# First MLP products inside the last pair of heads, and the first quarter of features in chunks of 384 tokens

## The chip, the cores and the metric

The kernel runs on one core of one Trainium2 chip. The metric is the time of one execution on the device in microseconds (us), median of several runs. TensorE (PE) multiplies into PSUM; VectorE (DVE), ScalarE (ACT) and GpSimd (POOL) do the elementwise work; SyncE's queue (SP) issues the DMAs. Each engine takes its instructions in order, and semaphores tie the engines to each other.

## The reference

Inputs are q, k and v of shape (2, 8, 768, 64), 16 centroids for each head, and two pairs of weight matrices of 512 x 2048 and 2048 x 512, all in float64. What is computed, cut to its core:

```
q_assign = argmax(q_n . c_n); k_assign = argmax(k_n . c_n)      # nearest of 16 centroids
scores = where(q_assign == k_assign, (q . k) / 8, -1e9)          # 768 x 768 for each of 16 heads
attn = softmax(scores) @ v                                       # (2, 8, 768, 64)
x = attn as (1536 tokens, 512)
h = relu(x @ w1_in); x = (h * h) @ w1_out                        # first MLP
h = x @ w2_in; x = (h * clip(h + 3, 0, 6) / 6) @ w2_out          # second MLP
```

## The kernel before

Attention goes by pairs of heads (a "unit", `NU` = 8: two batches of four pairs). A pair has 12 query tiles of 128 rows. For tile n, PE makes the scores `s` (L593, L596), DVE their maximum `nm` (L602), ACT the exponent `e` (L613); PE transposes `e` into `t` in two halves (L629), each is split into a rounded part `eh` and a rest `el` (either ACT L639 and DVE L640, or by way of a copy `et` on POOL, L154 and L637; the table `ON_POOL` says which), and for each three tiles PE multiplies `eh` and `el` with v into `a` (L656). The two halves of `a` are added in `emit_u` (ACT `tmp`, DVE `u`, L670); there is one buffer for `a`, so the next three tiles' product waits for that sum. Every float32 operand is such a sum of two, so an exact product is three matmuls.

The order in attention is written out by hand (`schedule`, within `tc.manual_schedule()`): tile n emits its transposes, the exponent of n+1 and the scores of n+2, and the tables `STEPS`, `FIRST`, `WEIGHTS`, `WEIGHTS_7` and `AV` put each preparing step of each pair at a place (tile, slot 0 to 4). Beside the tiles run the preparing steps of the next pair (transposes of q and k, clusters, one-hot `oh` and its transposed mask `toh` L459, the splitting of v) and the decoding of the first quarter of `w1_in`, one of eight pieces in a pair and two in the last.

The weights come as float64 and are decoded in seven instructions (`decode`): POOL clamps `t` (L167), ACT scales `u` (L169), DVE does three integer steps (L172, L174, L179), ACT rounds the high part (L183), and the low part is on POOL for the first quarter and on DVE for the others (L185).

The MLPs take 2048 features in four quarters and 1536 tokens in three chunks of 512. `mm1` makes 4 x 12 products of 512 columns and their gate (ACT `r` L842, `g` L843, POOL `gh` L154, DVE `gl` L848); `mm2` makes 4 x 12 products with the second matrix. The steps go mm1(0), mm1(1), mm2(0), mm1(2), mm2(1), and so on. `load_w` decodes a matrix in four pieces of 128 rows, with one buffer each for `t`, `u` and `a` and two for the raw `wr`; outside attention a scheduler sets the order at build time. The first of these is the first quarter of `w1_out`: its four pieces are decoded from the end of attention on, and mm2(0) needs all four.

Of the kernel before, what the change touches and what calls it, by code (L numbers as in the profile page):

```python
# [38 lines left out]
    "v0": (-6, 4),  # L39
    "v1": (-1, 2),  # L40
# [11 lines left out]
        "v0": (1, 4),  # L52
# [4 lines left out]
        "load v": (-6, 4),  # L57
        "k0": (-12, 2),
# [5 lines left out]
        "stack1": (-10, 3),  # L64
# [33 lines left out]
TMP_DVE = ()  # L98
BIG = float(2**60)
# [5 lines left out]
def cluster_attention_mlp_kernel(  # L105
# [50 lines left out]
    def decode(pool, hi, lo, r, on_dve):  # L156
# [42 lines left out]
    with ExitStack() as actx:  # L199
# [63 lines left out]
        def first_weights():  # L263
# [3 lines left out]
            def half(c, h):  # L267
# [19 lines left out]
            return [half(c, h) for c in range(4) for h in range(2)]  # L287
# [37 lines left out]
        def prep(u):  # L325
# [9 lines left out]
            def transp(x, half):  # L335
# [42 lines left out]
            def sims(half, x):  # L378
# [12 lines left out]
                if u == 0:  # L391
                    steps.insert(1, (C0, "H"))
# [5 lines left out]
                if x == 1 and u == 0:  # L398
# [27 lines left out]
            def leader(r0=0, r1=R, i=None):  # L426
# [9 lines left out]
                (nc.gpsimd if u else nc.vector).tensor_tensor(  # L436
# [3 lines left out]
            def onehot(r0=0, r1=R, i=None):  # L440
# [9 lines left out]
                nc.vector.tensor_tensor(  # L450
# [25 lines left out]
            def vsplit(half):  # L476
# [5 lines left out]
                pool_round(tt[:, :, 0:D], vr)  # L482
                nc.gpsimd.tensor_sub(tt[:, :, D:], vr, f(tt)[:, :, 0:D])
# [134 lines left out]
        def emit_tr(n, half):  # L618
# [27 lines left out]
        def emit_av(g, part):  # L646
# [7 lines left out]
            for kr in (2 * part, 2 * part + 1):  # L654
# [43 lines left out]
        def emit_norm(u, half):  # L698
# [20 lines left out]
            pool_round(XH[:, j, xs], xx)  # L719
            nc.gpsimd.tensor_sub(XL[:, j, xs], xx, f(XH)[:, j, xs])  # L720
# [13 lines left out]
        def schedule():  # L734
# [20 lines left out]
            for g in range(NTL // 3):  # L755
                for part in range(3):
# [32 lines left out]
    TC = 512  # L789
    NC = NT // TC  # L790
    NF = FQ // P
    ND = DM // P
    with ExitStack() as mctx:
        t_p = mctx.enter_context(tc.tile_pool(name="t", bufs=2, reuse_waits="tile"))
        g_p = mctx.enter_context(tc.tile_pool(name="g", bufs=2, reuse_waits="tile"))
# [3 lines left out]
        acc_p = mctx.enter_context(tc.tile_pool(name="acc", bufs=1, reuse_waits="tile"))  # L799
# [20 lines left out]

        acc = acc_p.tile([P, NC, 4, 512], F32, name="acc")
        G = {}

        def mm1(m, fq, c):
            wh, wl = wts[m, fq, 0]
            gh = g_p.tile([P, NF, TC], F32R, tag="gh", name="gh")
            gl = g_p.tile([P, NF, TC], F32R, tag="gl", name="gl")
            cs = slice(c * TC, c * TC + TC)
            for fb in range(NF):
                fs = slice(fb * P, fb * P + P)  # L830
                h = ps_h.tile([P, TC], F32, tag="h", name="h")
                n = 0
                for d in range(ND):
                    for w, x in ((wh, XH), (wh, XL), (wl, XH)):
                        nc.tensor.matmul(  # L835
                            h, w[:, d, fs], x[:, d, cs], start=(n == 0), stop=(n == 3 * ND - 1)
                        )
                        n += 1
                r = t_p.tile([P, TC], F32, tag="r", name="r")
                g = t_p.tile([P, TC], F32, tag="g", name="g")  # L840
                if m == 0:
                    nc.scalar.activation(r, h, AF.Relu)  # L842
                    nc.scalar.activation(g, r, AF.Square)  # L843
                else:
                    nc.scalar.activation(r, h, AF.Relu, bias=three)  # L845
# [91 lines left out]
```

## Time and profile before

| | |
|---|---|
| median of 3 runs | 811.45 us (810.27 to 814.22) |
| the profiled execution | 810.54 us, span 808.8 us |
| PE busy | 781.5 us, 97% of the span |
| DVE, ACT, POOL busy | 530.1, 395.8, 344.0 us |
| attention | 0 to 283.56 us of the span |
| both MLPs | 283.56 us to the end |

A busy PE is not PE at its peak: matmuls overlap, so their mean duration is longer than the time from one start to the next. A row of busy time by stretch gives the stretch, its length, the busy time of PE, PE's weight loads, DVE, ACT and POOL with their instructions, the granted clock as a share of 2.4 GHz (0.5 is 1.2 GHz), and the share and rate of the DMAs. Shares over the span mean little here, since attention and the MLPs have different limits; the rows below are read by stage.

### The profile page before, as it was taken

Reading aid. Unit: us, or ns where it says so; the run is one execution under the profiler, and the core shown is the slowest. Engines: PE = TensorE matmul, PEld = TensorE weight load, DVE = VectorE, ACT = ScalarE, POOL = GpSimd, SP = SyncE. Lnnn points to the kernel's source line nnn. Section 1 sums busy time; section 2 is a strip of 40 time slices with the busy share of each in tenths; the row PEclk is TensorE's granted clock in tenths of the full one; section 3 lists DMA queues with packets and bytes.
Section 4 is the critical chain, followed back from the end, with each engine's and each line's share of the span. In section 5 each row is a group of like instructions: output and inputs, shape, how many; then the busy total and the mean of one; then the engine's idle time right before and its main releaser. Section 6 shows DMA issues by size and latency. Waiting matters only on the chain.

```text
span 808.8 us, 11331 instructions
## 1 busy us (share of the span) xinstructions
PE 781.5 (97%) x3973; PEld 664.1 (82%) x3973; DVE 530.1 (66%) x877; ACT 395.8 (49%) x784; POOL 344.0 (43%) x461
## 2 busy tenths in 40 slices
PE   7999999999998699999999999999999999999998
PEld 6888888888987688888888888888888888888887
DVE  6888889898886666655766455576654666643432
ACT  5888888887886555545434334331333222311110
POOL 1778887888787552233322122333222221211110
PEclk9999999999999999999999999999999999999999
DMA  8837538448350123333222121121221211000012
GB/s 179 175 87 168 130 71 199 92 109 182 69 123 15 57 77 103 104 104 101 77 83 79 40 92 52 53 79 52 79 79 41 89 53 53 26 1 1 13 47 97
DMA packets 58536, 67.34 MB, mean 83 GB/s; under 512 B 41320, under 2 KB 41744, under 8 KB 58480
## 3 DMA queue, kind: packets, MB, share of 16 engines
q1 hardware_dynamic: 58480, 66.62, 30.8%
q8 instruction: 32, 0.52, 0.3%
q14 instruction: 24, 0.20, 0.1%
HBM read 43.02 MB, written 3.15 MB: 57 GB/s over the span
## 4 chain that ended last, share of the span: by engine, by line
PE 82%; POOL 5%; DVE 5%; issue 3%; ACT 2%; DMA 1%; SPq 1%; ACTq 0%; POOLq 0%
PE o L868 32%; PE h L835 32%; PE a L656 5%; PE t L629 4%; PE s L593 2%; PE s L596 2%; POOL el L637 2%; DVE nm L602 2%; PE tsim L394 2%; PE tq L349 1%; POOL eh L154 1%; DVE el L640 1%; DMA rawq<-in_q_dram 1%; DVE a L174 1%; DVE xx L718 1%
## 5 line engine op out<-in xcount | busy, mean ns | idle before, releaser
L835 PE MATMUL h<-xh,w 128*128 128x512 f32 x768 | 240.3, 389 | 0.0
L835 PEld LDWEIGHTS h<-xh,w 128*128 128x128 f32 x768 | 144.2, 188 | 29.7
L154 POOL TENSOR_SCALAR gh<-g 128x512 fp32r<-128x512 f32 x96 | 73.9, 769 | 194.1 <-DVE g L846 136.1
L835 PE MATMUL h<-xl,w 128*128 128x512 f32 x384 | 149.6, 390 | 0.0
L868 PE MATMUL o<-w,gh 128*128 128x512 f32 (+1 forms) x392 | 120.3, 385 | 0.0
L868 PE MATMUL o<-gh,w 128*128 128x512 f32 x384 | 120.2, 389 | 0.0
L167 POOL TENSOR_SCALAR t<-wr 128x512 f32<-128x512 f32 (+1 forms) x68 | 48.1, 707 | 161.9 <-DVE w L185 160.5
L183 ACT ACTIVATE w<-t 128x512 fp32r<-128x512 f32 (+1 forms) x68 | 41.2, 605 | 129.0 <-DVE t L179 90.6
L629 PE MATMUL t<-ident,e 128*128 128x128 f32 x576 | 93.6, 276 | 10.0 <-ACT e L613 8.4
L637 POOL TENSOR_TENSOR el<-et,eh 128x384 fp32r<-128x384 f32 x96 | 97.3, 1013 | 7.9
L848 DVE TENSOR_TENSOR gl<-g,gh 128x512 fp32r<-128x512 f32 x96 | 66.4, 693 | 51.5 <-POOL gh L154 51.5
L602 DVE TENSOR_REDUCE nm<-s 128x1 f32<-128x768 f32 x96 | 90.7, 946 | 2.2 <-PE s L596 2.2
L613 ACT ACTIVATE e<-s,nm 128x768 f32<-128x768 f32 x96 | 86.5, 901 | 5.3 <-DVE nm L602 5.3
L629 PEld LDWEIGHTS t<-ident,e 128*128 128x128 f32 x576 | 71.0, 141 | 21.5 <-ACT e L613 13.5
L169 ACT ACTIVATE u<-t 128x512 f32<-128x512 f32 (+1 forms) x68 | 41.3, 607 | 93.4 <-POOL t L167 93.4
L868 PEld LDWEIGHTS o<-w,gh 128*128 128x128 f32 x392 | 73.2, 188 | 14.7
L835 PEld LDWEIGHTS h<-xl,w 128*128 128x128 f32 x384 | 72.1, 188 | 14.9
L868 PEld LDWEIGHTS o<-gh,w 128*128 128x128 f32 x384 | 72.1, 188 | 14.9
L845 ACT ACTIVATE r<-h,three 128x512 f32<-128x512 f32 x48 | 32.6, 682 | 89.9 <-PE h L835 89.9
L868 PE MATMUL o<-w,gl 128*128 128x512 f32 (+1 forms) x196 | 75.4, 385 | 0.0
L172 DVE TENSOR_SCALAR a<-u 128x512 int32<-128x512 int32 (+1 forms) x68 | 30.9, 454 | 67.6 <-ACT u L169 67.6
L868 PE MATMUL o<-gl,w 128*128 128x512 f32 x192 | 74.7, 389 | 0.0
(121 smaller groups left out, 1298.5 us busy)
## 6 DMA issues: line engine op xcount, KB each, us to landing
wr<-in_moe_w_out_dram SPq DMA_DIRECT2D x32, 512.0 KB
wr<-in_moe_w_in_dram SPq DMA_DIRECT2D x28, 512.0 KB
op<-H SPq DMA_DIRECT2D x56, 192.0 KB
op<-L SPq DMA_DIRECT2D x28, 192.0 KB
rawv<-in_v_dram SPq DMA_DIRECT2D x16, 192.0 KB
out_dram<-acc SPq DMA_DIRECT2D x11, 256.0 KB
rawq<-in_q_dram SPq DMA_DIRECT2D x14, 192.0 KB
rawk<-in_k_dram SPq DMA_DIRECT2D x14, 192.0 KB
```

The source lines that it names most:

```text
L154: nc.gpsimd.tensor_scalar(dst, src, 1.0, 0.0, op0=ALU.mult, op1=ALU.add)
L167: nc.gpsimd.tensor_scalar(t, f(hw), MOST, -MOST, op0=ALU.min, op1=ALU.max)
L169: nc.scalar.activation(u, t, AF.Copy, scale=2.0**-112)
L183: nc.scalar.activation(hi, t, AF.Copy)
L602: nc.vector.tensor_reduce(nm, S_t[n][:, :, :HS], axis=AX.XY, op=ALU.max, negate=True)
L613: nc.scalar.activation(e, s[:, :, :HS], AF.Exp, bias=nm, accum_out=sums[u][:, i * R + r : i * R + r + 1])
L629: nc.tensor.transpose(t[:, c, :], E_t[n][:, half, c * P : (c + 1) * P], ident)
L637: nc.gpsimd.tensor_sub(el, et, f(eh))
L656: nc.tensor.matmul(a[:, :HS], vs[:, kr, i, :], x[:, kr, :], start=(kr == 0 and x is eh), stop=(kr == R - 1 and x is el),)
L835: nc.tensor.matmul(h, w[:, d, fs], x[:, d, cs], start=(n == 0), stop=(n == 3 * ND - 1))
L848: nc.vector.tensor_sub(gl[:, fb], g, f(gh)[:, fb])
L868: nc.tensor.matmul(o, lhsT, rhs, start=(n == 0), stop=(n == 3 * NF - 1))
```

## The change

The first 384 tokens' products with the first quarter of `w1_in` (4 blocks of 12 products, and their gates) are emitted among the tiles of the last pair, at the places of `EARLY`. The first quarter of features then goes by four chunks of 384 tokens. The steps are now early(0); mm1(384); mm1(768), mm2(0), mm2(384); mm1(1152), mm2(768); mm1 of the next quarter; and so on. Half the columns of all four row blocks of `w1_in` are decoded first. In all pairs the step `u` of this decoding is on DVE; the last two pieces have their clamp and low part on DVE and `u` on ACT. The last pair has its own `ON_POOL_LAST` (9 halves on POOL instead of 12, four of whose copies are on DVE); the other pairs have 11 instead of 12. H and L are one tile, and the accumulator lies by features for the first MLP and by tokens for the second. The switches `E_...` and `SIM3` other than `E_U` stand as the code was. Slots of the preparing steps move by one or two tiles at most.

```
+    "load v": (-12, 4),
...
-WEIGHTS = ((0, 4), (3, 0), (4, 0), (5, 0), (5, 3), (7, 1), (7, 4), (9, 1))
+WEIGHTS = ((0, 2), (3, 4), (4, 4), (6, 0), (6, 3), (7, 3), (9, 3), (10, 0))
...
-    ((-2, 4), (0, 2), (0, 4), (1, 3), (2, 2), (3, 3), (3, 4), (4, 1)),
+    ((-1, 3), (0, 0), (0, 4), (1, 1), (1, 3), (1, 4), (2, 0), (2, 0)),
...
-AV = ((4, 0), (4, 4), (5, 2))
+LATE = {(2, 1), (3, 1)}
+EARLY = (
+    ((2, 1), (2, 4), (3, 1)),
+    ((5, 3), (5, 4), (6, 1)),
+    ((7, 1), (7, 4), (9, 0)),
+    ((9, 1), (10, 1), (10, 4)),
+)
+
+AV = ((3, 3), (3, 4), (4, 4), (5, 0), (5, 2), (5, 2))
...
 ON_POOL = {
-    (0, 0), (0, 1), (1, 1), (2, 1), (3, 1), (4, 1), (6, 0), (7, 0), (9, 0), (9, 1), (10, 0),
-    (11, 1),
+    (0, 0), (1, 0), (1, 1), (2, 1), (4, 0), (4, 1), (6, 0), (7, 0), (9, 0), (9, 1), (11, 1),
...
-ET_DVE = {
-    (2, 0), (5, 0), (7, 1), (10, 0), (10, 1),
+ET_DVE = set()
+ON_POOL_LAST = {
+    (0, 0), (2, 0), (4, 0), (5, 0), (6, 1), (8, 0), (8, 1), (9, 0), (10, 0),
 }
+ET_DVE_LAST = {
+    (2, 0), (5, 0), (6, 1), (10, 0),
+}
...
-        nc.gpsimd.tensor_scalar(t, f(hw), MOST, -MOST, op0=ALU.min, op1=ALU.max)
+        (nc.vector if clamp_on_dve or not on_dve and E_CLAMP == "v" else nc.gpsimd).tensor_scalar(
+            t, f(hw), MOST, -MOST, op0=ALU.min, op1=ALU.max
+        )
         yield
-        nc.scalar.activation(u, t, AF.Copy, scale=2.0**-112)
+        if on_dve or E_U == "a":
+            nc.scalar.activation(u, t, AF.Copy, scale=2.0**-112)
+        else:
+            nc.vector.tensor_scalar(u, t, 2.0**-112, None, op0=ALU.mult)
...
-        (nc.vector if on_dve else nc.gpsimd).tensor_sub(lo, t, f(hi))
+        (nc.vector if on_dve or E_LO == "v" else nc.gpsimd).tensor_sub(lo, t, f(hi))
...
-            return [half(c, h) for c in range(4) for h in range(2)]
+            return [half(c, h) for h in range(2) for c in range(4)]
...
-            if (n % (2 * R), half) in ON_POOL:
+            if (n % (2 * R), half) in (ON_POOL if u < NU - 1 else ON_POOL_LAST):
-                copy((n % (2 * R), half) in ET_DVE, et, t)
+                copy((n % (2 * R), half) in (ET_DVE if u < NU - 1 else ET_DVE_LAST), et, t)
...
-            for kr in (2 * part, 2 * part + 1):
+            for kr in (part,):
...
+        def emit_early(fb, part):
+
+            if early[0] is None:
+                g = hl_p.tile([P, 2, NF, HS], F32R, tag="HL", name="g0")
+                early[0] = (g[:, 0], g[:, 1])
+            if part == 0:
+                early[1][fb] = ps_t.tile([P, 512], F32, tag="t", name="h0")
+            h = early[1][fb][:, :HS]
+            if part < 2:
+                for d in (2 * part, 2 * part + 1):
+                    products(h, w_first[:, 0], w_first[:, 1], fb, d, slice(0, HS))
+            else:
+                t = raw_p.tile([P, 2, HS], F32, tag="raw" + "qk"[fb % 2], name="rg")
+                gate(0, h, t[:, 0], t[:, 1], early[0][0][:, fb], early[0][1][:, fb])
...
+            for fb, places in enumerate(EARLY):
+                for part, w in enumerate(places):
+                    at(w, T * (NU - 1), partial(emit_early, fb, part))
...
+                n = HS if (m, fq) == (0, 0) else TC
+                steps += [(m, fq, c, n) for c in range(0, NT, n)]
...
             if s:
+                mm1(m, fq, c, n)
+            if s == 2:
+                mm2(*steps[0])
+            if s > 1:
                 mm2(*steps[s - 1])
```

`products` holds the three matmuls of one row block of `mm1`, and `gate` the four instructions of its gate; `emit_early` calls both.

On POOL, in the last pair, around the two halves of the pair before that are rounded there (`xh`, `xl`); `wr` and `w` are the first quarter's raw and decoded weights. Before:

```order
L637 TENSOR_TENSOR el<-et,eh 128x3x128
L154 TENSOR_SCALAR xh<-xx 128x384
L720 TENSOR_TENSOR xl<-xx,xh 128x384
L185 TENSOR_TENSOR w_68<-t,w_68 128x256
L154 TENSOR_SCALAR eh<-et 128x3x128
L637 TENSOR_TENSOR el<-et,eh 128x3x128
L154 TENSOR_SCALAR xh<-xx 128x384
L720 TENSOR_TENSOR xl<-xx,xh 128x384
L167 TENSOR_SCALAR t<-wr_3793 128x256
L154 TENSOR_SCALAR eh<-et 128x3x128
L637 TENSOR_TENSOR el<-et,eh 128x3x128
```

Now (`g` is the gate's rounded part of the early products):

```order
L178 TENSOR_SCALAR g_3751<-rg 128x384
L178 TENSOR_SCALAR eh<-et 128x3x128
L694 TENSOR_TENSOR el<-et,eh 128x3x128
L178 TENSOR_SCALAR xh<-xx 128x384
L780 TENSOR_TENSOR xl<-xx,xh 128x384
L178 TENSOR_SCALAR xh<-xx 128x384
L780 TENSOR_TENSOR xl<-xx,xh 128x384
L178 TENSOR_SCALAR eh<-et 128x3x128
L694 TENSOR_TENSOR el<-et,eh 128x3x128
L178 TENSOR_SCALAR g_3751<-rg 128x384
L178 TENSOR_SCALAR eh<-et 128x3x128
```

The low part and the clamp of the weights, which stood between the two, are gone from POOL, and a gate's rounding stands there.

On ACT, across the end of attention (`tmp` is the half of `a` that frees its buffer, `rb` the last pair's row factors, `u<-t 128x512` and `w<-t 128x512` the first piece of `w1_out`). Before:

```order
L613 ACTIVATE e,sums<-s,nm 128x768
L639 ACTIVATE eh<-t 128x3x128 x2
L169 ACTIVATE u<-t 128x512
L151 ACTIVATE tmp<-a 64x384
L151 ACTIVATE et<-t 128x384
L151 ACTIVATE tmp<-a 64x384
L710 ACTIVATE rb<-ri 128x384
L183 ACTIVATE w<-t 128x512
L710 ACTIVATE rb<-ri 128x384
L169 ACTIVATE u<-t 128x512
L842 ACTIVATE r<-h 128x512
L843 ACTIVATE g<-r 128x512
```

Now:

```order
L696 ACTIVATE eh<-t 128x3x128
L175 ACTIVATE tmp<-a 64x384
L696 ACTIVATE eh<-t 128x3x128
L175 ACTIVATE tmp<-a 64x384
L767 ACTIVATE rb<-ri 128x384
L196 ACTIVATE u<-t 128x512
L767 ACTIVATE rb<-ri 128x384
L238 ACTIVATE r<-h 128x384
L239 ACTIVATE g<-r 128x384
L238 ACTIVATE r<-h 128x384
L239 ACTIVATE g<-r 128x384
L212 ACTIVATE w<-t 128x512
```

The first piece's `u` stood ahead of both `tmp` and now stands behind both; two whole gates (`r`, `g`) now stand ahead of its `w`.

On PE, where the second products begin (`o`, one of four blocks of 128 features; `g0` is the early gate). Before:

```order
L868 MATMUL o_4446<-gl_4291,w_4143 128x512
L868 MATMUL o_4446<-gh_4290,w_4143 128x512 x2
L868 MATMUL o_4446<-gl_4291,w_4143 128x512
L868 MATMUL o_4446<-gh_4290,w_4143 128x512
L868 MATMUL o_4460<-gh_4290,w_4143 128x512
L868 MATMUL o_4460<-gl_4291,w_4143 128x512
L868 MATMUL o_4460<-gh_4290,w_4143 128x512 x2
```

Now:

```order
L231 MATMUL h_4473<-xh_63,w0_68 128x384
L937 MATMUL o_4492<-g0_3751,w_4189 128x384 x9
L937 MATMUL o_4506<-g0_3751,w_4189 128x384 x9
L937 MATMUL o_4492<-g0_3751,w_4189 128x384 x2
L937 MATMUL o_4506<-g0_3751,w_4189 128x384 x2
L937 MATMUL o_4492<-g0_3751,w_4189 128x384
L937 MATMUL o_4506<-g0_3751,w_4189 128x384
L937 MATMUL o_4520<-g0_3751,w_4189 128x384 x12
L937 MATMUL o_4534<-g0_3751,w_4189 128x384 x12
```

Nine products of the second block now stand ahead of the last three of the first, which need the fourth piece of `w1_out`.

## Rows read from the trace of the kernel before

**Rows 1.** Page, part 1: busy time of each engine

```profile
PE 781.5 (97%) x3973; PEld 664.1 (82%) x3973; DVE 530.1 (66%) x877; ACT 395.8 (49%) x784; POOL 344.0 (43%) x461
```

**Rows 2.** Busy time by stretch: a middle pair, the last stretch, the MLPs

```profile
193.93:226.08 32.15, 30.69 (x205) 27.88 (x204) 27.98 (x48) 27.21 (x62) 26.93 (x36) 1.00 0.56 127
226.08:283.56 57.48, 47.04 (x280) 41.86 (x278) 41.30 (x68) 38.47 (x87) 41.32 (x55) 0.94 0.21 56
283.56:808.00 524.44, 522.23 (x2318) 432.70 (x2317) 298.80 (x469) 173.50 (x290) 130.11 (x171) 1.00 0.20 64
```

**Rows 3.** Busy time by stretch, within the last stretch

```profile
249.24:252.44 3.20, 3.20 (x11) 3.16 (x12) 2.58 (x4) 1.70 (x4) 1.51 (x2) 0.51 0.00 0
...
262.52:265.83 3.31, 0.00 (x1) 0.00 (x0) 0.10 (x1) 1.73 (x5) 2.16 (x4) 1.00 0.00 0
265.83:269.53 3.70, 3.70 (x14) 3.56 (x15) 2.17 (x4) 2.19 (x5) 2.26 (x3) 0.54 0.00 0
...
274.83:283.56 8.73, 6.31 (x38) 5.41 (x36) 6.01 (x9) 3.48 (x8) 6.64 (x9) 1.00 0.33 113
```

**Rows 4.** Waits, 226.08 to 283.6 us: total, times, longest us

```profile
ACT u L169 <- POOL t L167: 6.3, 3, 2.9
PE t L629 <- ACT e L613: 6.1, 3, 3.3
...
PE a L656 <- DVE u L670: 2.1, 1, 2.1
```

**Rows 5.** Chain of waits, 255 to 284 us: start us, us, what

```profile
261.02 1.01 POOL el L637
...
262.59 0.99 POOL xl L720
...
263.67 0.41 POOL t L167
...
264.90 0.89 ACT e L613 x2
```

**Rows 6.** Timeline of ACT, end of attention: start us, us, what, [idle before <-releaser]

```profile
274.83 0.91 ACT L613 ACTIVATE e<-s,nm 128x768 f32<-128x768 f32 x1
...
278.87 0.63 ACT L169 ACTIVATE u<-t 128x512 f32<-128x512 f32 x1 [1.81 <-POOL t L167]
```

**Rows 7.** Timeline of PE, products of 384 and of 512 columns, first second product

```profile
281.06 0.34 PE L656 MATMUL a<-el,vs 128*128 128x384 f32 x1
...
281.75 0.33 PE L656 MATMUL a<-el,vs 128*128 128x384 f32 x1
...
302.06 0.62 PE L835 MATMUL h<-xh,w 128*128 128x512 f32 x2
...
304.10 0.62 PE L835 MATMUL h<-xh,w 128*128 128x512 f32 x2
...
305.00 0.39 PE L868 MATMUL o<-gh,w 128*128 128x512 f32 x1
```

**Rows 8.** Timeline of DVE: low parts of the first and fourth piece of w1_out

```profile
285.21 0.69 DVE L185 TENSOR_TENSOR w<-t,w 128x512 fp32r<-128x512 f32 x1 [0.38 <-ACT w L183]
...
303.83 0.69 DVE L185 TENSOR_TENSOR w<-t,w 128x512 fp32r<-128x512 f32 x1
```

**Rows 9.** Waits, 97.5 to 226.08 us (four middle pairs): total, times, longest us

```profile
PEld L459 <- DVE oh L450: 5.6, 4, 1.4
```

**Rows 10.** Groups by line and form: out<-in xcount | busy us, mean ns

```profile
L639 ACT ACTIVATE eh<-t 128x384 fp32r<-128x384 f32 x96 | 47.0, 489 | 16.0 <-PE t L629 13.9
...
L179 DVE SCALAR_TENSOR_TENSOR t<-u,a 128x512 int32<-128x512 int32 x60 | 46.9, 782 | 3.4 <-DVE a L174 0.5
...
L174 DVE SCALAR_TENSOR_TENSOR a<-wr,a 128x512 int32<-128x512 int32 x60 | 41.8, 697 | 1.3
...
L172 DVE TENSOR_SCALAR a<-u 128x512 int32<-128x512 int32 x60 | 26.4, 440 | 67.6 <-ACT u L169 67.6
...
L174 DVE SCALAR_TENSOR_TENSOR a<-wr,a 128x256 int32<-128x256 int32 x8 | 8.3, 1034 | 0.0
```

More of the change, by code (lines that the diff above doesn't have):

```diff
@@ L38 @@
     "mask": (-5, 4),
-    "v0": (-6, 4),
-    "v1": (-1, 2),
+    "v0": (-5, 2),
+    "v1": (-3, 4),
     "rinv": (11, 0),
@@ L98 @@
 TMP_DVE = ()
+ET_DVE_LAST = {
+    (2, 0), (5, 0), (6, 1), (10, 0),
+}
+SIM3 = False
+E_OH = "v"
+E_W = "p"
+E_CLAMP = "p"
+E_LO = "p"
+E_U = "v"
+E_VH = "p"
+E_VL = "p"
+E_XH = "p"
+E_XL = "p"
 BIG = float(2**60)
@@ L193, in w_src, with products, gate @@
         return w.rearrange("(c p) f -> p c f", p=P)
+    TC = 512
+    NF = FQ // P
+    ND = DM // P
+    def products(h, wh, wl, fb, d, cs):
+        fs = slice(fb * P, fb * P + P)
+        for n, (w, x) in enumerate(((wh, XH), (wh, XL), (wl, XH))):
+            nc.tensor.matmul(
+                h, w[:, d, fs], x[:, d, cs],
+                start=(d == 0 and n == 0), stop=(d == ND - 1 and n == 2),
+            )
+    def gate(m, h, r, g, gh, gl):
+        if m == 0:
+            nc.scalar.activation(r, h, AF.Relu)
+            nc.scalar.activation(g, r, AF.Square)
+        else:
+            nc.scalar.activation(r, h, AF.Relu, bias=three)
+            nc.vector.scalar_tensor_tensor(g, r, 6.0, h, op0=ALU.min, op1=ALU.mult)
+        pool_round(gh, g)
+        nc.vector.tensor_sub(gl, g, f(gh))
     w0_p = ctx.enter_context(tc.tile_pool(name="w0", bufs=1))
@@ L397, in sims @@
                     )
-                if x == 1 and u == 0:
+                if x == 1 and (u == 0 or SIM3):
                     nc.scalar.activation(st["sim"][:, hs], t[0:64, :HS], AF.Copy)
@@ L755, in schedule @@
             for g in range(NTL // 3):
-                for part in range(3):
+                for part in range(6):
                     at(AV[part], 3 * g, partial(emit_av, g, part))
@@ L819, in load_w, with mm1, mm2 @@
             wts[m, fq, which] = (hi, lo)
-        acc = acc_p.tile([P, NC, 4, 512], F32, name="acc")
-        G = {}
-        def mm1(m, fq, c):
+        acc = acc_p.tile([P, 4, NT], F32, name="acc")
+        acc1 = acc.rearrange("p d t -> p (d t)").rearrange("p (b n) -> p b n", n=DM)
+        G = {(0, 0, 0): early[0]}
+        def mm1(m, fq, c0, n):
             wh, wl = wts[m, fq, 0]
-            gh = g_p.tile([P, NF, TC], F32R, tag="gh", name="gh")
-            gl = g_p.tile([P, NF, TC], F32R, tag="gl", name="gl")
-            cs = slice(c * TC, c * TC + TC)
+            gh = g_p.tile([P, NF, TC], F32R, tag="gh", name="gh")[:, :, :n]
+            gl = g_p.tile([P, NF, TC], F32R, tag="gl", name="gl")[:, :, :n]
             for fb in range(NF):
-                fs = slice(fb * P, fb * P + P)
-                h = ps_h.tile([P, TC], F32, tag="h", name="h")
-                n = 0
+                h = ps_h.tile([P, TC], F32, tag="h", name="h")[:, :n]
                 for d in range(ND):
[L834 to L845, printed above, removed]
-                    nc.vector.scalar_tensor_tensor(g, r, 6.0, h, op0=ALU.min, op1=ALU.mult)
-                pool_round(gh[:, fb], g)
-                nc.vector.tensor_sub(gl[:, fb], g, f(gh)[:, fb])
-            G[m, fq, c] = (gh, gl)
-        def mm2(m, fq, c):
+                    products(h, wh, wl, fb, d, slice(c0, c0 + n))
+                r = t_p.tile([P, TC], F32, tag="r", name="r")[:, :n]
+                g = t_p.tile([P, TC], F32, tag="g", name="g")[:, :n]
+                gate(m, h, r, g, gh[:, fb], gl[:, fb])
+            G[m, fq, c0] = (gh, gl)
+        def mm2(m, fq, c0, n):
             wh, wl = wts[m, fq, 1]
-            gh, gl = G.pop((m, fq, c))
+            gh, gl = G.pop((m, fq, c0))
             last = fq == FF // FQ - 1
@@ L856, in mm2 @@
                 ds = slice(db * P, db * P + P)
-                end = last and m == 1 and (c, db) == (NC - 1, 3)
-                for ns in (slice(0, 256), slice(256, 512)) if end else (slice(0, 512),):
+                end = last and m == 1 and (c0 + n, db) == (NT, 3)
+                if m == 0:
+                    pieces = (slice(0, n),)
+                else:
+                    pieces = (slice(0, 256), slice(256, 512)) if end else (slice(0, 512),)
+                for ns in pieces:
                     o = ps_o.tile([P, 512], F32, tag="o", name="o")[:, ns]
-                    n = 0
+                    k = 0
                     for fb in range(NF):
@@ L889, in mm2 @@
                         )
-        steps = [(m, fq, c) for m in range(2) for fq in range(FF // FQ) for c in range(NC)]
+        steps = []
+        for m in range(2):
+            for fq in range(FF // FQ):
+                n = HS if (m, fq) == (0, 0) else TC
+                steps += [(m, fq, c, n) for c in range(0, NT, n)]
         load_w(0, 0, 1)
-        for s, (m, fq, c) in enumerate(steps):
+        for s, (m, fq, c, n) in enumerate(steps):
             if c == 0:
```

84 lines of the change are left out of this document (45 added, 39 removed).

## Prediction

> **What bounds the kernel now.** I read the page first: PE is busy for 97% of the span [rows 1], so only PE's own work and the few microseconds in which it stands still can give time back. The table by stretch says where these are [rows 2]. From 283.56 us on, PE is busy for 522.23 of 524.44 us: the MLPs are bound by PE alone. In a middle pair it is busy for 30.69 of 32.15 us. In the last stretch, 226.08 to 283.56 us, it is busy for 47.04 of 57.48 us at a mean clock of 0.94: 10.4 us without work. Within it [rows 3] there is a gap of 3.31 us, two stretches of 3.20 and 3.70 us at half clock (0.51 and 0.54, the 1.2 GHz level; the second follows the gap directly), and the tail from 274.83 us. The slow stretches cost 3.20 x 0.49 + 3.70 x 0.46 = 3.3 us, so 13.7 us could be had there.
>
> The waits tell why [rows 4]: ACT stood 6.3 us for POOL's clamp of the weights (L167), and PE 6.1 us for exponents behind it on ACT. The chain shows one such case whole [rows 5]: POOL works off a pair's rest `el` and the rounding `xh`, `xl` of the pair before, only then comes the clamp at 263.67, and ACT, which takes its list in order, starts the next exponent at 264.90. In the tail ACT waits again, 1.81 us, for the clamp of the first piece of `w1_out`, with the copy `tmp` behind it that frees PE's accumulator [rows 6]; PE then waits 2.1 us for DVE's `u` [rows 4].
>
> **The change part by part.** *Products moved.* One product of 512 columns takes (304.10 - 302.06) / 9 = 0.2267 us, one of 384 takes (281.75 - 281.06) / 4 = 0.1725 us [rows 7]. The MLPs have 2304 products, 522.3 us. Now 2016 of them keep 512 columns (457.0 us) and 384 have 384 (66.2 us): 0.9 us more in all. But 48 of these, 8.3 us, go into attention. What PE has to do after attention falls by 522.3 - 457.0 - 66.2 + 8.3 = **7.4 us**.
>
> *The last pair.* Removed from POOL there: three of twelve halves (0.5 + 1.0 us each), two clamps and two low parts; added: four gate roundings. The clamp that ACT waited for [rows 5] is on DVE now, and the order shows nothing left between `xl` and the next half on POOL but a gate's rounding. Of PE's 13.7 us I leave a middle pair's share idle, (32.15 - 30.69) / 32.15 x 57 = 2.6 us, and 1.2 us for the last wait for `u`, which remains, though `tmp` no longer stands behind the clamp. That gives 9.9 us back, and 8.3 us of new products go in: attention ends **1.6 us** earlier. The bounds are wide: all 13.7 us back would be 5.4 us earlier, nothing back 8.3 us later. A second reckoning agrees: DVE, the next engine, gets three more `el`, three more copies and four `gl` (0.55 us each, as for ACT's 0.489 [rows 10] or a little more), two clamps and two low parts (some 0.4): 7.1 us on its 41.3 [rows 2]. At a middle pair's share of 27.98 / 32.15 = 0.87, 48.4 us of DVE take 55.6 us, 1.9 less than now. Between ends so far apart I take the value from PE.
>
> *A wait added: the first piece of `w1_out`.* Before, its `u` ran at 278.87 [rows 6], before attention's end, and its low part was done at 285.21 + 0.69 = 285.90, 2.3 us after that end; the fourth was done at 303.83 + 0.69 = 304.52 [rows 8], and the second products began at 305.00 [rows 7]. They were just in time. Now `u` stands behind the last `tmp` and a row factor, so it starts about 1.1 us after the end of attention (two ACT instructions of 0.489) and takes 0.63; three integer steps of 0.44, 0.70 and 0.78 [rows 10], with one product for the last pair between, bring it to 4.2; the two gates that now stand ahead of `w` on ACT (four of 0.489) end there too; `w`, a `gl` and the low part end at 6.0, or 3.7 later than before. The three further pieces took 304.52 - 285.90 = 18.6 us beside seven gates of 512; with narrower gates I take 17.4. The fourth is done at 23.4, its high part 0.8 earlier at 22.6. PE comes sooner: 86 products (ten of the 96 fill the last wait of attention in the new order), six transposes (0.6, an estimate from the 384 columns each three cover) and the 18 second products that don't need the fourth piece make 14.8 + 0.6 + 3.1 = 18.5. So PE stands for 4.1 us where it stood for none, with everything of both MLPs behind it. A slow clock may follow: after 3.31 us of rest PE lost 1.7 us, after the 2.1 us in the tail the clock stayed at 1.00 [rows 3]. I count 1.3: **5.4 us** lost. Bounds: 0 if the pieces come in time, 9 if each takes a microsecond longer and the clock falls. Later matrices have the time of three chunks each, so I cost them at nothing.
>
> *Steps in other slots, all pairs.* The list of DVE around the one-hot is nearly what it was; the shift of a weight piece (1.034 us [rows 10]) stands behind the one-hot now and the scaling `u` (some 0.4 us) ahead of it. PE waits 1.4 us for it in each pair [rows 9]. If 0.6 us of this goes in six pairs, 3.6 us; since the shift then delays the next maximum, I take half, **1.8 us** earlier. Bounds: 8.4 us earlier (all of it), 2.5 us later (0.42 us more on DVE in each). The products with v in six steps, one tile for H and L, and the accumulator's new order change neither an instruction's size nor what PE waits for; cover is PE's own queue, and without it a move is worth one product, 0.17 us.
>
> The sum: -7.4 - 1.6 + 5.4 - 1.8 = -5.4 us on the profiled execution's 810.54 us (span 808.8 and 1.7 around it): **805.2 us**. That execution was 0.9 us under the median of the runs, 811.45, so the same sum on the median is 806.0.
>
> **The rivals.** (a) *The decoding keeps up.* It did before, with 0.5 us to spare [rows 7, 8]; if the gates of 384 let the pieces pass in 4 us, nothing is lost there: 805.2 - 5.4 = 799.8. Against it: the first piece starts 3.7 us later.
> (b) *The early products push instead of filling.* Their weights' last piece is finished within the same tiles, each holds one of the three buffers that the transposes use, and their gates stand ahead of exponents on ACT. If only half of the 9.9 us comes back, 810.2: no change.
> (c) *DVE becomes the bound of the last pair; slower than before.* The 256-element shift in attention takes 1.034 us, longer than twice as many elements in the MLPs (0.697) [rows 10], so DVE already loses time beside a busy POOL. Six moved instructions, four `gl` and two low parts, may lose a POOL instruction of 1.0 us each [rows 5], and each `gl` waits in DVE's list for POOL's rounding, 1.5 us behind a half there. Then DVE has 41.3 + 7.1 + 6 + 6 = 60.4 us, at 0.87 that is 69.4 us, attention ends 11.9 us later instead of 1.6 earlier, and the time is 818.7. It is slower by over 0.5% from an end of attention at 292.2 us on. For it speaks DVE's share; against it, that DVE had 16 us free in this stretch.
> The Trainium skill ("SBUF — State Buffer", section "SBUF: two separate sides") says that a Vector instruction with two SBUF inputs and a GpSimd instruction that reads SBUF share one pair of ports as an exclusive lock, so that the loser waits for the whole instruction. By that rule all six would be exposed, and (c)'s first 6 us would be real; the trace's 1.034 against 0.697 agrees with it, as a mean.
> (d) *The slots give more:* the whole wait for the one-hot goes, 805.2 - 6.6 = 798.6.
>
> **How the numbers follow.** Chances: forecast 0.50 (its own range 801.5 to 808.5), (a) 0.20, (b) 0.16, (c) 0.09, (d) 0.05. I call 0.5% (4.1 us) what can be told from no change: faster is below 807.4, slower above 815.5. Faster: 0.41 of the forecast's 0.50, with (a) and (d): 0.66. Same: the rest of the forecast and (b): 0.25. Slower: (c), 0.09. The range from 797.5 to 811 leaves out (c) and the ends of (a) and (d).
>
> **What would show it.** In the profile after: attention's last product with v at about 282 us; 48 products `h0` between the tiles of the last pair and no wait of ACT for POOL's clamp there; a gap of about 4 us on PE some 18 us after that, ended by ACT's `w` of the fourth piece, with a clock near 0.5 behind it; PE without gaps from there on; a middle pair of 31.5 to 32.2 us. The prediction is wrong in its main term if that gap is under 1 us or over 7, in its second if attention ends before 278 or after 287 us, and in its fourth if a middle pair differs by more than 0.8 us.

## The result and the profile after

The changed kernel takes 803.33 us (median of 4 runs, 801.34 to 805.96), the kernel before in the same session 811.55 us: ratio 0.9896, 95% interval 0.9855 to 0.9938. The forecast was 805.2 (806.0 on the median), so sign and rough size are right; the parts are not. The medians lie 8.2 us apart, the profiled executions only 4.6: that of the changed kernel, 805.96 us (span 804.3), was the slowest of its four. The parts are those of the two profiled executions:

| part of the span | forecast | measured |
|---|---|---|
| start to the last one-hot mask (slots) | -1.8 | 232.17 to 227.35: -4.8 |
| from there to the last product with v | -1.6 | 51.39 to 51.16: -0.2 |
| from there to the end (MLPs) | -7.4 + 5.4 = -2.0 | 525.2 to 525.8: +0.6 |
| sum | -5.4 | -4.5 |

The kernel before from its last one-hot mask to its last product with v:

```profile
232.17:283.56 51.39, 42.11 (x247) 37.54 (x247) 35.24 (x58) 33.36 (x75) 35.48 (x48) 0.93 0.13 39
```

The table by stretch of the changed kernel (stretch, length, busy PE, weight loads, DVE, ACT, POOL, clock, DMA) answers to [rows 2, 3]. Two middle pairs, the last pair, the MLPs' first products, the stretch with two gaps, and what follows it:

```profile
102.51:133.38 30.87, 30.65 (x204) 27.77 (x203) 27.57 (x49) 26.99 (x62) 25.39 (x34) 1.00 0.63 133
164.43:196.58 32.15, 31.10 (x204) 27.67 (x203) 27.50 (x49) 26.98 (x62) 25.37 (x34) 1.00 0.55 124
227.35:278.51 51.16, 48.29 (x301) 44.01 (x300) 39.81 (x70) 36.58 (x82) 30.98 (x41) 1.00 0.12 37
278.51:294.45 15.94, 15.94 (x93) 15.38 (x93) 11.11 (x18) 10.09 (x20) 9.08 (x11) 1.00 0.21 67
294.45:302.03 7.58, 3.83 (x20) 2.87 (x19) 5.67 (x10) 3.73 (x8) 3.03 (x4) 0.96 0.30 83
302.03:306.00 3.97, 3.97 (x12) 3.97 (x13) 2.39 (x4) 0.63 (x1) 0.66 (x1) 0.50 0.29 106
306.00:315.00 9.00, 9.00 (x46) 8.74 (x46) 3.15 (x6) 3.80 (x8) 0.64 (x1) 0.87 0.33 100
```

A middle pair takes 30.87 us where it took 32.15: PE no longer stands there. (The pair from 164.43 on is as long as before; in it PE stood for the next pair's mask, see experiment 3.) In the last pair PE is busy for 48.29 of 51.16 us and the clock is full, yet it is no shorter. After attention PE has no gap until 294.45; then it stands twice, and the clock falls to the 1.2 GHz level. PE's timeline (start, us, what, idle before and releaser) shows both waits, for `w` of the third and the fourth piece of `w1_out`:

```profile
278.34 0.34 PE L713 MATMUL a<-el,vs 128*128 128x384 f32 x1
...
294.45 1.20 PE L937 MATMUL o<-g,w 128*128 128x384 f32 x6
296.75 2.73 PE L937 MATMUL o<-g,w 128*128 128x384 f32 x12 [1.10 <-ACT w L212]
302.03 1.33 PE L937 MATMUL o<-g,w 128*128 128x384 f32 x3 [2.54 <-ACT w L212]
```

In the kernel before the second products began at 305.00 us, just behind the fourth piece [rows 7, 8], and PE was busy for 522.23 of the MLPs' 524.44 us [rows 2]. ACT's timeline shows the first piece as the prediction had it: `u` behind `tmp` and a row factor, then two gates, then `w`, 5.0 us after attention's end:

```profile
278.71 0.49 ACT L175 ACTIVATE tmp<-a 64x384 f32<-64x384 f32 x1 [4.10 <-PE a L713]
279.10 0.51 ACT L767 ACTIVATE rb<-ri 128x384 f32<-128x384 f32 x1
279.51 0.62 ACT L196 ACTIVATE u<-t 128x512 f32<-128x512 f32 x1
...
281.99 0.53 ACT L239 ACTIVATE g<-r 128x384 f32<-128x384 f32 x1
...
283.51 0.63 ACT L212 ACTIVATE w<-t 128x512 fp32r<-128x512 f32 x1
```

### The profile page after: what moved, and what is told of

Read it like the earlier page. It is cut to its first block, busy times and chain, and to the rows that moved or that the text cites. A ratio compares the mean times of both kernels' runs of the same rounds, so it can differ in the third digit from the quotient of the medians.

```text
span 804.3 us, 11576 instructions
## 1 busy us (share of the span) xinstructions
PE 784.9 (98%) x4069; PEld 676.4 (84%) x4069; DVE 531.7 (66%) x897; ACT 396.6 (49%) x794; POOL 324.9 (40%) x441
## 4 chain that ended last, share of the span: by engine, by line
PE 82%; DVE 4%; DMA 4%; ACT 3%; POOL 3%; issue 2%; SPq 2%; ACTq 0%; DVEq 0%; POOLq 0%
PE o L937 33%; PE h L231 30%; PE a L713 6%; PE t L686 5%; DMA op<-HL 3%; PE s L650 3%; PE s L653 2%; PE tsim L446 1%; SPq L298 1%; DVE nm L659 1%; POOL el L694 1%; ACT et L175 1%; DVE el L697 1%; DMA op<-mt 1%; PE tq L401 1%
## 5 line engine op out<-in xcount | busy, mean ns | idle before, releaser
L231 PE MATMUL h<-xh,w 128*128 128x512 f32 (+1 forms) x800 | 245.3, 382 | 0.5 <-ACT et L175 0.5
L231 PEld LDWEIGHTS h<-xh,w 128*128 128x128 f32 x800 | 149.3, 188 | 27.0 <-ACT et L175 0.7
L231 PE MATMUL h<-xl,w 128*128 128x512 f32 (+1 forms) x400 | 152.3, 381 | 0.0
L178 POOL TENSOR_SCALAR gh<-g 128x512 fp32r<-128x512 f32 (+1 forms) x96 | 70.5, 734 | 193.9 <-DVE g L242 133.5
L937 PE MATMUL o<-gh,w 128*128 128x512 f32 (+1 forms) x384 | 115.2, 376 | 0.0
L244 DVE TENSOR_TENSOR gl<-g,gh 128x512 fp32r<-128x512 f32 (+1 forms) x96 | 65.2, 680 | 54.5 <-POOL gh L178 54.5
L694 POOL TENSOR_TENSOR el<-et,eh 128x384 fp32r<-128x384 f32 x86 | 89.1, 1036 | 7.2
L231 PEld LDWEIGHTS h<-xl,w 128*128 128x128 f32 x400 | 75.1, 188 | 13.0
L713 PE MATMUL a<-eh,vs 128*128 128x384 f32 x192 | 71.2, 371 | 1.2 <-DVE u L727 1.2
L937 PE MATMUL o<-gl,w 128*128 128x512 f32 (+1 forms) x192 | 72.1, 376 | 0.0
```

The costliest lines, as they stand in the source:

```text
L178: nc.gpsimd.tensor_scalar(dst, src, 1.0, 0.0, op0=ALU.mult, op1=ALU.add)
L231: nc.tensor.matmul(h, w[:, d, fs], x[:, d, cs], start=(d == 0 and n == 0), stop=(d == ND - 1 and n == 2),)
L244: nc.vector.tensor_sub(gl, g, f(gh))
L694: nc.gpsimd.tensor_sub(el, et, f(eh))
L713: nc.tensor.matmul(a[:, :HS], vs[:, kr, i, :], x[:, kr, :], start=(kr == 0 and x is eh), stop=(kr == R - 1 and x is el),)
L937: nc.tensor.matmul(o, lhsT, rhs, start=(k == 0), stop=(k == 3 * NF - 1))
```

## The experiments

Each median stands beside that of the kernel before from the same session; "last stretch" is from the last one-hot mask to the last product with v.

**1. The shift back ahead of the one-hot.**

```
-WEIGHTS = (..., (4, 4), (6, 0), (6, 3), (7, 3), ...)
+WEIGHTS = (..., (4, 4), (5, 0), (5, 3), (7, 3), ...)
```

> The changed kernel with one edit: the two integer steps of the weight piece stand where they stood before the change, so that the shift (DVE a<-wr) is ahead of the one-hot again in each middle pair; nothing else moves. Theory A (the shift's place is what made PE wait for the one-hot): the wait of some 1.2 us returns in each of six pairs, a middle pair takes about 32.0 us instead of 30.8, and the time is 5 to 7 us over the changed kernel. Rival B (the wait went because u left ACT and POOL has one half fewer): a middle pair stays at 30.8 us and the time within 1 us.

Measured: 803.85 us (ratio 0.9908, 0.9878 to 0.9937), the changed kernel's time; a middle pair takes 30.84 us. My theory fell in this kernel: the shift ahead of the one-hot costs nothing.

```profile
132.95:163.79 30.84, 30.73 (x204) 27.76 (x203) 27.86 (x49) 26.86 (x62) 25.36 (x34) 1.00 0.58 134
```

**2. The same move alone, in the kernel before.**

```
-WEIGHTS = (..., (4, 0), (5, 0), (5, 3), (7, 1), ...)
+WEIGHTS = (..., (4, 0), (6, 0), (6, 3), (7, 1), ...)
```

> The kernel before with one edit: the two integer steps of the weight piece at the changed kernel's places, the shift behind the one-hot. Theory A: a middle pair falls from 32.15 to about 31 us, and the time is 5 to 7 us under the kernel before (about 805.5). Rival B: no change from 811.5.

Measured: 807.39 beside 811.02 us (ratio 0.9952, 0.9932 to 0.9972), a middle pair 31.34 us, 0.8 less. There the place does count, though for less than the 5 to 7 us of theory A. In the trace the last stretch became 1.9 us longer, at a mean clock of 0.87 instead of 0.93:

```profile
133.92:165.26 31.34, 30.84 (x205) 27.79 (x204) 27.32 (x48) 26.98 (x62) 26.57 (x36) 1.00 0.56 124
227.96:281.27 53.31, 44.99 (x248) 40.60 (x248) 35.92 (x59) 34.21 (x77) 36.37 (x49) 0.87 0.17 49
```

Between the two kernels the difference lies in how long the shift ahead of the one-hot is. In the kernel before, on POOL and DVE:

```profile
132.43 1.05 POOL L720 TENSOR_TENSOR xl<-xx,xh 128x384 fp32r<-128x384 f32 x1
```
```profile
132.58 1.19 DVE L174 SCALAR_TENSOR_TENSOR a<-wr,a 128x256 int32<-128x256 int32 x1
...
135.13 0.56 DVE L450 TENSOR_TENSOR oh<-iota,mn 128x384 bf16<-128x384 f32 x1
```

The shift starts 0.15 us into POOL's `xl` and ends 0.29 after it. In experiment 1 it starts just ahead of `xl`, and takes 0.41; it is POOL's instruction that is stretched a little:

```profile
130.56 0.41 DVE L203 SCALAR_TENSOR_TENSOR a<-wr,a 128x256 int32<-128x256 int32 x1
```
```profile
130.72 1.13 POOL L780 TENSOR_TENSOR xl<-xx,xh 128x384 fp32r<-128x384 f32 x1
```

**5. The shift one place up, in the kernel before.** This tests the collision by itself: the shift stays ahead of the one-hot but meets another POOL instruction.

```
-WEIGHTS = (..., (4, 0), (5, 0), (5, 3), (7, 1), ...)
+WEIGHTS = (..., (4, 0), (5, 0), (5, 2), (7, 1), ...)
```

> The kernel before with one edit: the shift of the weight piece one place up in DVE's list, ahead of the rest el instead of behind it; it is still ahead of the one-hot. Theory A (the shift is long only because it starts while POOL's xl runs and has to wait for the end of it; one place up it starts beside xh): the shift takes some 0.41 us instead of 1.19, a middle pair some 31.4 us instead of 32.15, and the time falls by 3 to 4 us as with the shift behind the one-hot, to about 807.5. Rival B (what counts is that the shift stands ahead of the one-hot at all, or that DVE is busy): the shift keeps its length and the time stays at 811.

Measured: 811.96 beside 812.10 us, no change. But the trace does not speak for rival B:

```profile
131.91 0.66 DVE L174 SCALAR_TENSOR_TENSOR a<-wr,a 128x256 int32<-128x256 int32 x1
...
134.39 1.03 DVE L450 TENSOR_TENSOR oh<-iota,mn 128x384 bf16<-128x384 f32 x1
```
```profile
131.62 0.68 POOL L154 TENSOR_SCALAR xh<-xx 128x384 fp32r<-128x384 f32 x1
...
134.01 0.99 POOL L637 TENSOR_TENSOR el<-et,eh 128x384 fp32r<-128x384 f32 x1
```

The shift is 0.53 us shorter, and the one-hot, which now runs earlier, meets POOL's `el`: it ends 0.42 us after `el` and takes 1.03 instead of 0.56. So it is in all pairs; the groups by form of experiment 5 (count, busy, mean ns), where the kernel before has 1034 for the shift [rows 10]:

```profile
L450 DVE TENSOR_TENSOR oh<-iota,mn 128x384 bf16<-128x384 f32 x7 | 7.2, 1027 | 0.2
L174 DVE SCALAR_TENSOR_TENSOR a<-wr,a 128x256 int32<-128x256 int32 x8 | 4.8, 603 | 0.0
```

In the changed kernel the shift's mean is 703, in experiment 1 it is 447. What a moved DVE instruction gives depends on which POOL instruction it then meets. The Trainium skill ("SBUF — State Buffer", section "SBUF: two separate sides") says that whichever of the two starts first keeps the shared ports for its whole instruction. These rows agree: the later one ends after the earlier one has.

**3. No early products,** chunks of 512 and their steps as before; everything else as changed.

```
-EARLY = (((2, 1), (2, 4), (3, 1)), ...)
+EARLY = ()
...
-                n = HS if (m, fq) == (0, 0) else TC
+                n = TC
...
-            if s:
-                mm1(m, fq, c, n)
-            if s == 2:
-                mm2(*steps[0])
-            if s > 1:
+            mm1(m, fq, c, n)
+            if s:
                 mm2(*steps[s - 1])
```

> The changed kernel without the early products: no first product inside the last pair, three chunks of 512 for the first features as before the change; the slots, the tables of the last pair and the weights' steps stay as changed. Theory A (the early products fill waits): the last pair ends nearly where it does now, at 276 to 279 us of the span, the MLPs take 522 us after it without a gap, and the time is 803 to 806. Rival B (they push, since the tables alone took the waits away): attention ends at 270 to 272 us and the time is 797 to 799.

Measured: 796.85 beside 811.02 us (ratio 0.9829, 0.9797 to 0.9860), 6.5 us under the changed kernel (6.0 if each is taken against the kernel before of its own session). Rival B holds in the time; attention ends at 274.86 us in this trace, not at 270 to 272, since its pairs were long (below). The last stretch:

```profile
233.41:274.86 41.45, 39.01 (x246) 34.81 (x246) 37.18 (x66) 32.52 (x74) 28.32 (x37) 1.00 0.15 45
```

The other edits alone shorten the last stretch from 51.39 to 41.45, by 9.9 us, and the early products lengthen it again by 9.7, more than the 8.3 us that they take: nothing was left to fill. This profiled execution was the slowest of its kernel, 803.07 us (the others 794.98 to 797.54). In four pairs PE stood for the next pair's mask to come by DMA; in one of them, 34.3 us long, the clock fell behind a wait of 1.06 us (mean 0.95). Its waits from 40 to 240 us:

```profile
PE s L648 <- DMA op<-mt: 3.9, 4, 1.3
PEld s L648 <- DMA op<-mt: 2.7, 2, 1.6
```

In the kernel before this wait was 0.3 us in all; the long pair of the changed kernel has one of 0.5 us:

```profile
171.84 0.59 PE L653 MATMUL s<-op 80*128 80x384 f32 x2 [0.52 <-DMA op<-mt]
```

What makes the masks late is not shown. It is not the shorter pair alone: in experiment 1, with pairs of 30.84 us, PE has no such wait.

**6. No early products, but chunks of 384.** Against experiment 3:

```
-                n = TC
+                n = HS if (m, fq) == (0, 0) else TC
```

> The changed kernel without early products, but the first quarter of features still in four chunks of 384 tokens, all after attention. Theory A (the chunks cost next to nothing themselves; the gap before the second products comes only because the early products let PE arrive sooner): no gap, attention ends as without early products, and the time is 0.5 to 2 us over the kernel without early products and with chunks of 512 (796.9), some 5 us under the changed kernel. Rival B (the narrow chunks themselves bring the loss): 801 or more.

Measured: 804.51 beside 812.10 us (ratio 0.9903, 0.9879 to 0.9927): no gain over the changed kernel. My reckoning was wrong: two narrow chunks keep PE busy for 96 x 0.173 = 16.6 us ahead of the second products, two wide ones for 21.8. So the same gaps come back:

```profile
286.36 0.41 PE L932 MATMUL o<-gh,w 128*128 128x384 f32 x1 [0.59 <-ACT w L207]
291.62 0.41 PE L932 MATMUL o<-gh,w 128*128 128x384 f32 x1 [2.94 <-ACT w L207]
```

The cause of the gaps is thus the work that stands ahead of the second products, whether early products or narrow chunks shorten it. The last stretch is as short as in experiment 3, and the MLPs take 533.6 us after it, 7.8 more than in the changed kernel: with narrow chunks the early products neither gain nor lose, and the loss against experiment 3 comes with the narrow chunks.

```profile
226.01:267.46 41.45, 38.97 (x247) 34.90 (x247) 37.15 (x66) 32.57 (x74) 28.29 (x37) 1.00 0.15 45
```

**4. Two buffers for the decoding steps.**

```
-        wd_p = mctx.enter_context(tc.tile_pool(name="wd", bufs=1, reuse_waits="tile"))
+        wd_p = mctx.enter_context(tc.tile_pool(name="wd", bufs=2, reuse_waits="tile"))
```

> The changed kernel with two buffers instead of one for the steps t, u and a of the matrices decoded outside attention. Theory A (PE's gaps of 1.1 and 2.5 us before the second products come from the four pieces of w1_out going one behind the other, and the half clock of some 6 us behind them comes from these gaps): both go, 6 to 7 us of the profiled execution, and the median falls by 3 to 5 us, to 798 to 800. Rival B (the lists of ACT and DVE or the raw loads set the pace): the fourth piece is no more than 1 us earlier and the time is the same.

Measured: 804.59 beside 811.02 us (ratio 0.9919, 0.9895 to 0.9943): the same. Neither theory holds whole: the fourth piece is done 18.9 us after attention's end instead of 23.5, and the first gaps shrink from 3.64 to 1.71 us, but another comes, for the accumulator's copy behind more weight pieces in ACT's list:

```profile
298.11 0.62 PE L937 MATMUL o<-g,w 128*128 128x384 f32 x2 [1.47 <-ACT w L212]
298.97 8.25 PE L937 MATMUL o<-g,w 128*128 128x384 f32 x37 [0.24 <-DVE w L214]
310.28 0.66 PE L937 MATMUL o<-gh,w 128*128 128x384 f32 x1 [2.35 <-ACT acc L945]
```

**8. Second products behind the fourth chunk.**

```
-        g_p = mctx.enter_context(tc.tile_pool(name="g", bufs=2, reuse_waits="tile"))
+        g_p = mctx.enter_context(tc.tile_pool(name="g", bufs=3, reuse_waits="tile"))
...
-            if s == 2:
-                mm2(*steps[0])
-            if s > 1:
+            if s == 3:
+                for p in range(3):
+                    mm2(*steps[p])
+            if s > 3:
                 mm2(*steps[s - 1])
```

> The changed kernel with the early products kept, three buffers for the gates' outputs instead of two, and the first second products put behind the fourth chunk's first products, so that PE has 25 us of work while w1_out is decoded (now 16). Theory A (the gaps and the half clock behind them are what the early products cost in the MLPs): both go, the MLPs take 516 us after attention instead of 522.6, and the time falls by 4 to 6 us to about 798. Rival B (the wait comes back at another place, as with two buffers): within 1.5 us of the changed kernel's 803.3. In neither does attention end earlier.

Measured: 806.15 beside 812.10 us (ratio 0.9917, 0.9894 to 0.9939): rival B in its mechanism, though the median is 2.8 us over the changed kernel's 803.3 (2.3 by sessions) and not within 1.5. The scheduler put the decoding later too (first `w` at 287.29, 10.0 us after attention's end instead of 5.0), and PE waits at three places:

```profile
305.08 7.53 PE L937 MATMUL o<-g,w 128*128 128x384 f32 x39 [1.83 <-ACT w L212]
315.13 0.49 PE L231 MATMUL h<-xh,w 128*128 128x512 f32 x1 [1.82 <-ACT w L212]
317.71 0.66 PE L937 MATMUL o<-gh,w 128*128 128x384 f32 x1 [2.08 <-ACT acc L945]
```

Whether early products would pay in the MLPs with `w1_out` decoded sooner is left open.

**7, 9, 10 and 11. What made the last stretch shorter.** Experiment 7 gives experiment 3 the other pairs' table in the last pair:

```
-ON_POOL_LAST = {(0, 0), (2, 0), ...}
+ON_POOL_LAST = ON_POOL
-ET_DVE_LAST = {(2, 0), (5, 0), (6, 1), (10, 0)}
+ET_DVE_LAST = ET_DVE
```

> The changed kernel without early products and with chunks of 512, and in the last pair the table of the other pairs: 11 halves on POOL and no copies on DVE, instead of 9 and four; the clamp and the low part of the last two weight pieces stay on DVE. Theory A (the table of the last pair gave back the waits there): the last pair takes 4 to 8 us longer than with its own table (41.3 us), 801 to 805. Rival B (the clamp and the low part on DVE did it alone): within 1 us of 796.9.

Experiment 9 is the kernel before with `u` on DVE, 10 has the shift's move of experiment 2 as well:

```
-        nc.scalar.activation(u, t, AF.Copy, scale=2.0**-112)
+        if on_dve:
+            nc.scalar.activation(u, t, AF.Copy, scale=2.0**-112)
+        else:
+            nc.vector.tensor_scalar(u, t, 2.0**-112, None, op0=ALU.mult)
```

> The kernel before with one edit: the scaling u of the weights decoded in attention is on DVE instead of ACT, in all pairs; clamp and low part stay on POOL. Theory A (the last pair is long because ACT, which makes the exponents, stands for POOL's clamp): the last stretch, 51.4 us from its one-hot to the last product with v, becomes 4 to 7 us shorter, and the time is 805 to 807. Rival B (the wait only changes its engine: DVE, which makes the maxima, stands for the same clamp): the last stretch stays within 1.5 us and the time at 811 to 812.

> The kernel before with two edits: u on DVE as in the run beside it, and the shift of the weight piece behind the one-hot as in the second run. Theory A: both gains add up, middle pairs of 31 to 31.4 us and a last stretch of 45 to 47 us, 801 to 803; then most of what the whole change brings without its early products (796.9) comes from these two edits. Rival B: u on DVE gives nothing in the last pair or takes the place of the shift ahead of the one-hot, 807 to 809.

Experiment 11 is 7 with the clamp and the low part of the last two pieces on POOL, and with that their `u` on DVE:

```
-LATE = {(2, 1), (3, 1)}
+LATE = set()
```

> The changed kernel without early products, with the other pairs' table in the last pair, and now also with the clamp and the low part of the last two weight pieces on POOL (their u on DVE like the others). Theory A (it is the clamp and the low part that POOL no longer has which made the last pair 41 to 42 us): the last stretch becomes 3 to 7 us longer and the time 801 to 804. Rival B (u leaving ACT is enough, or the new slots are): within 1.5 us of the 797.9 with them on DVE.

The last stretch of 7, 9, 10 and 11, and the medians:

```profile
228.85:271.39 42.54, 39.57 (x247) 34.66 (x247) 36.01 (x60) 33.91 (x78) 31.83 (x41) 1.00 0.15 44
```
```profile
232.00:278.70 46.70, 39.82 (x246) 34.59 (x247) 35.66 (x60) 32.66 (x73) 35.79 (x48) 1.00 0.15 43
```
```profile
225.71:272.92 47.21, 40.10 (x246) 34.60 (x247) 36.37 (x61) 33.16 (x75) 36.75 (x49) 1.00 0.16 46
```
```profile
227.17:274.02 46.85, 40.99 (x247) 36.05 (x247) 35.00 (x58) 33.57 (x76) 33.65 (x45) 0.96 0.14 40
```

| | median, us | before, same session | ratio (95%) |
|---|---|---|---|
| 7 | 797.88 | 812.10 | 0.9819 (0.9794 to 0.9844) |
| 9 | 806.82 | 811.54 | 0.9942 (0.9925 to 0.9960) |
| 10 | 801.25 | 811.54 | 0.9871 (0.9850 to 0.9893) |
| 11 | 802.21 | 811.54 | 0.9892 (0.9867 to 0.9916) |

Experiment 7 speaks for its rival B, 9, 10 and 11 for their theory A (the last stretch of 10 lies 0.2 us over its 45 to 47).

With `u` on DVE alone (9) the last stretch falls from 51.39 to 46.70. DVE then stands for POOL's clamp as ACT did [rows 4], nearly as long in all, but PE's wait for exponents falls from 6.1 to 3.4 us; waits of 9's last stretch:

```profile
DVE u L172 <- POOL t L167: 5.5, 2, 3.1
PE t L632 <- ACT e L616: 3.4, 3, 1.7
```

With all new slots but the clamp on POOL (11) it is 46.85; with clamp and low part on DVE (7) 42.54; with the table too (3) 41.45. So in these traces `u` gives 4.7 us, clamp and low part 4.3, the table 1.1 and no time that can be told apart. Part of it is the clock: the mean of 0.93 before is 1.00 in experiment 9, where PE is busy 2.3 us less for the same products and idle 2.4 us less; the 0.96 of experiment 11 is 1.00 in 7, with 1.4 us less busy and 2.9 less idle. In experiment 10 `u` and the shift's place add up: 10.3 us, where 9 and 2 gave 4.7 and 3.6.

**12. The kernel before with three edits.** Experiment 10, and the clamp and low part of the last two pieces on DVE.

```
+                        end = c == 3
                         st["d"] = decode(
-                            wd0_p, w_first[:, 0, c, hs], w_first[:, 1, c, hs], st["r"], False
+                            wd0_p, w_first[:, 0, c, hs], w_first[:, 1, c, hs], st["r"], end, end
                         )
```

> The kernel before with three edits: u on DVE, the shift behind the one-hot, and for the last two weight pieces the clamp and the low part on DVE (with their u on ACT, as in the changed kernel). Tables, slots, products and chunks else as before. Theory A (these three carry the change; early products, narrow chunks and the other slots bring nothing): the last stretch falls from 47.0 us to 42 to 43, and the time from 801.3 to 796 to 798, as the changed kernel without early products has it. Rival B (the last pair's new slots are needed too): 799 or more.

Measured: 798.82 beside 812.29 us (ratio 0.9831, 0.9807 to 0.9855):

```profile
226.20:270.25 44.05, 39.78 (x246) 34.60 (x247) 36.43 (x63) 33.64 (x77) 34.58 (x45) 1.00 0.17 50
132.80:163.96 31.16, 30.83 (x204) 27.80 (x205) 27.90 (x49) 26.99 (x61) 26.68 (x36) 1.00 0.59 129
```

Between A and B: the last stretch is 1.5 us over experiment 7's, which the last pair's other slots could give (not tested), and a middle pair takes 31.16 us. Three edits beat the whole change, and by ratio stand level with experiments 3 and 7; experiment 3 has the lowest median of all.

## Why the prediction was right, and where it was wrong

- **Products moved, -7.4, and the wait for `w1_out`, +5.4.** The wait came where it was put (first `w` starts 5.0 us after attention's end against 4.2, the fourth ends 23.5 after it against 22.6), as two gaps of 1.10 + 2.54 = 3.6 us against 4.1. The slow clock behind it was sized too small for this execution: 3.97 x 0.50 + 9.00 x 0.13 = 3.2 us against 1.3. Both together, 6.8, eat nearly all of the 7.4, and the MLPs end up 0.6 us longer instead of shorter; some 1 us of that has no term (experiment 3, with neither gap nor slow clock there, also takes 0.9 us more than before). The slow clock differs between executions: in experiment 1, whose MLPs have the same gaps, it cost 2.50 x 0.19 + 2.50 x 0.50 = 1.7 us, and the MLPs took 524.4 us, 0.9 less than before. There the wait and the clock together cost 5.4 us, as forecast.

```profile
294.92 2.73 PE L937 MATMUL o<-g,w 128*128 128x384 f32 x12 [1.12 <-ACT w L212]
300.19 7.06 PE L937 MATMUL o<-g,w 128*128 128x384 f32 x30 [2.54 <-ACT w L212]
```
```profile
300.00:302.50 2.50, 2.31 (x11) 2.23 (x12) 0.91 (x2) 0.77 (x2) 0.65 (x1) 0.81 0.48 184
302.50:305.00 2.50, 2.50 (x9) 2.50 (x8) 1.67 (x4) 0.63 (x1) 0.00 (x0) 0.50 0.20 48
```

- **The last pair, -1.6.** The 9.9 us that I had given back were met to the decimal (experiment 3), but that is luck, since my reasons were not right: 4.7 come from `u` leaving ACT, which I named only as a wait of ACT, and the table of halves, which I put first, gives 1.1. The step that failed is "8.3 us of new products go in": they cost 9.7, and the stretch ends 0.2 earlier, not 1.6.
- **Slots in all pairs, -1.8.** This is the term most mis-sized: 1.3 us a pair and 4.8 in all (6.7 in experiment 1, whose trace has no long pair), near rival (d) and outside the 0.8 us that I had allowed. The step that failed is "I take half": I gave the shift's place 0.6 us a pair and halved that for a delay of the next maximum, while experiment 2 has 0.8 us a pair net of any delay. I saw the shift and its unusual 1.034 us [rows 10], and used the rule behind it only for rival (c); that the wait of 1.4 us [rows 9] was in good part this collision I did not see. The rest I put at nothing: `u` on DVE gives 0.2 us a pair (31.97 us in experiment 9), and the 0.3 us between the 31.16 us of experiment 12 and the changed kernel's 30.87 must lie in the other slots and tables, which no run tested one by one.
- **The rivals.** (a) did not happen: the gaps are there. (b) named what the early products do in the last pair, but not that the other edits alone would give 9.9. (c) did not happen: DVE was busy for 39.81 of 51.16 us.

That the profiled time came out right is luck: the slots' 3.0 us too little stood against 2.6 too much in the MLPs and 1.4 in the last pair. Three moves in the decoding of the weights (`u` to DVE, the shift behind the one-hot, clamp and low part of the last two pieces to DVE) give, in the kernel before, more than the whole change (experiment 12); in the changed kernel one of them, the shift's, can be undone without loss (experiment 1), since the shift meets `xl` otherwise there. The change's first part, the early products with their narrow chunks, costs about 6 us (experiment 3).

## What to carry to other kernels

Work moved into an engine's idle time pays only if that time is still idle after the other edits: reckon each part alone, and what it triggers downstream (here the weights' decoding, which two wide chunks just covered). When an instruction's mean is far above its like, look what runs on the other engine as it starts; a move by one place can end the collision or hand it to the neighbour.

## What was not expected of the hardware

- An instruction of DVE with both inputs in SBUF (none in PE's PSUM) that starts while POOL works ends only after POOL's instruction, so that the same shift takes 0.41 to 1.19 us and the same one-hot 0.56 to 1.03 (kernel before, experiments 1 and 5). The other way round, POOL's `el` takes 1.34 instead of 0.99 us where it starts 0.07 us behind the one-hot (changed kernel). DVE's `el`, one input of which is PE's `t` in PSUM, is not held so: in the kernel before, of 61 that started at least 0.15 us before the end of a POOL instruction, 18 ended before it, but none of the 23 shifts and third integer steps (`t<-u,a`).
- After a gap of 2.54 us on PE the clock stood at the 1.2 GHz level for about 6 us in the changed kernel, and for about 3.4 us in experiment 1. The length of the gap alone does not say whether the clock falls: the wait of 2.1 us at the end of attention left it full in the kernel before [rows 3, 4] and in experiments 9 and 10, while in 2 and 5 a stretch at a clock of 0.50 followed it, as one followed a wait of 1.06 us in experiment 3.
